# When the first remainders of q and k are loaded, and by which queue, and four norms a group sooner, in a fused attention and MLP kernel

## The chip, the core and the metric

The kernel runs on one core of one Trainium2 chip. The core has five engines that run side by side, each through its own instructions in order: TensorE (PE, matrix products into PSUM; its weight loads are listed apart as PEld), VectorE (DVE), ScalarE (ACT), GpSimd (POOL) and SyncE (SP, which here only issues transfers). Transfers between the chip's memory (HBM) and the on-chip memory are issued by SP, ACT or POOL and carried out by 16 DMA engines. The metric is the device time of one execution in microseconds (us). A profile shows one execution: its times count from the start of its span, and its lines name lines of the kernel (L184 is line 184).

## The reference

Attention over normalised q and k, and then a two-layer network over the joined heads. q, k and v have the shape (8 batches, 12 heads, 448 tokens, 64), in float32; `tau` is 0.1; the layers are 768 to 2048 and back.

```python
q_n = q / (np.linalg.norm(q, axis=-1, keepdims=True) + 1e-06)
k_n = k / (np.linalg.norm(k, axis=-1, keepdims=True) + 1e-06)
scores = np.matmul(q_n, k_n.transpose(0, 1, 3, 2)) / tau
scores = scores - np.max(scores, axis=-1, keepdims=True)
attn = np.exp(scores)
attn = attn / (np.sum(attn, axis=-1, keepdims=True) + 1e-09)
attn_out = np.matmul(attn, v)
x = attn_out.transpose(0, 2, 1, 3).reshape(B * S, H * D)
h = x @ w_in
out = np.maximum(0.01 * h, h) @ w_out
```

## The kernel before, in words

**Tiles.** The unit of attention is a slot: a pair of heads of one batch, six slots to a batch, 48 in all, numbered `s`. The 448 tokens of a head are 384 in three tiles of 128 (the main part) and a remainder of 64. The main part of q or k of a pair is one load of 192 KB. The remainder of q goes to partitions 0 to 63 of a fourth tile and that of k to partitions 64 to 127, in loads of 32 KB each, so that q with both remainders is 128x512 and k 128x384. The six slots of the first batch have a buffer of their own, `raw0`, filled by `load_first` (`part` 0 is the main part at L129, 1 the remainder at L134; `s0` and `n` say which slots). Later slots take turns in four buffers named `qk`, filled by `load_qk` with four loads on SP (L144, L145, L147 twice).

**One slot's way.** Squares (`squares`, L184, on POOL; for the first two slots on ACT and DVE, L522 to L533), sums over 64 (`sums`, L195, DVE), square roots as exp of half a log (`roots`, L202 and L203, ACT; L205 adds a small number for the first two slots), the norm (`normalise`: L214, L215 and two L219 on DVE, which write `qn` in bf16), transposes to `qkT` (on PE, L233, with a copy at L257 or L547 up to slot 9; from slot 10 by a DMA transpose on SP, L251), scores (L276, PE), exp (L288, ACT, into `pe`, and `pr` for the remainders of two slots together). Four heads then form a quarter `j` of a batch: `totals` (sums of exp by products with ones, L316; L329 and L330 invert them), `products` with v (L316, weights `v_b`, `v_rem`), `scale` (L351) into `xT`.

**The network.** `xT` of two batches is worked off in chunks of 384 and 512 tokens. `first` makes one of 16 groups of hidden columns (L374, PE) and its activation (L381, ACT, `hT`); `two_groups` and `second` make the output products (L453, L411).

**The order.** It is written out by hand: each engine runs the instructions in the order in which the program calls them, and waits by semaphores. First the loads are issued, then 22 products of ones (`fill`, L503) keep PE at work. A loop over the six slots of the first batch follows (L553 on): within step `s` come scores of `s`, sums of `s + 2`, the norm of `s + 1`, loads, `hold`, squares of `s + 3`, loads of weights and v, transposes of `s + 1`. `hold` (L510) is a copy of one element on POOL: POOL waits there for what it reads, and what POOL issues afterwards is issued no earlier. The first one reads the main part of k of slot 1. The software loads on POOL are `load_w_in` (L106), `load_w_out` (L113), `load_v` (L162, `v_b`) and `load_v_rem` (L169).

**Loads and semaphores.** The loads issued by SP and ACT take eight semaphores in turn. A load that takes one in use waits, on its engine, until the earlier load has landed; in the program before, the first to do so is the q load of slot 3, which waits for that of slot 0.

**The later part.** For each batch `b`: `visit` (output products of chunk `b`, with the scores of the next batch's slots in between; it begins with the scores of the remainders, for the slots 1 and 3 of that batch and their predecessors), `attend_batch(b + 1)`, loads of v, and `firsts(b + 1, 0, between)`. `between` says which sums and norms come ahead of which of the 16 groups. `norm(s)` is roots, norm, transposes, the load of slot `s + 4`, a hold and the squares of slot `s + 2`. The case `b == 0` has a list of its own, for slots 12 to 15 and the sums of 16.

Of the kernel before, what the change touches and what calls it, by code (L numbers as in the profile page):

```python
# [16 lines left out]
def kernel(  # L17
# [10 lines left out]
    nc = tc.nc  # L28
# [38 lines left out]
    gp = nc.gpsimd  # L67
# [50 lines left out]
    def main(x, b, h0, nh):  # L118
        return x[b, h0 : h0 + nh, 0:MAIN].rearrange("h (p t) d -> p h t d", t=3)

    raw0 = cpool.tile([128, NPAIR, 2, 7, D], F32, name="raw0")
    raw = {s: (raw0[:, s, :, 0:4], raw0[:, s, :, 4:7]) for s in range(NPAIR)}

    def load_first(eng, x, part, s0, n):

        h0, i = 2 * s0, 0 if x is q else 1
        if part == 0:
            dst = raw0[:, s0 : s0 + n, :, 4 * i : 4 * i + 3]
            eng.dma_start(  # L129
                out=dst.rearrange("p s h t d -> p (s h) t d"), in_=main(x, 0, h0, 2 * n)  # L130
            )
        else:
            dst = raw0[64 * i : 64 * i + 64, s0 : s0 + n, :, 3]
            eng.dma_start(  # L134
                out=dst.rearrange("p s h d -> p (s h) d"),
                in_=x[0, h0 : h0 + 2 * n, MAIN:S].rearrange("h p d -> p h d"),
            )

    def load_qk(s):
        if s >= NSLOT:  # L140
            return
        b, h0 = s // NPAIR, 2 * (s % NPAIR)
        both = ldp.tile([128, 2, 7, D], F32, name="qk")
        nc.sync.dma_start(out=both[:, :, 0:3], in_=main(q, b, h0, 2))  # L144
        nc.sync.dma_start(out=both[:, :, 4:7], in_=main(k, b, h0, 2))  # L145
        for i, x in enumerate((q, k)):
            nc.sync.dma_start(  # L147
                out=both[64 * i : 64 * i + 64, :, 3],
                in_=x[b, h0 : h0 + 2, MAIN:S].rearrange("h p d -> p h d"),
            )  # L150
        raw[s] = (both[:, :, 0:4], both[:, :, 4:7])
# [5 lines left out]
    def load_v(j):  # L157
        if j >= B * NQ:
            return
        b, jj = divmod(j, NQ)  # L160
        vb[j] = vbp.tile([128, 4, 3, D], BF16, name="v_b")
        gp.dma_start(out=vb[j], in_=main(v, b, 4 * jj, 4))  # L162

    def load_v_rem(b, parts=slice(0, 4)):
        if b >= B:
            return
        x = vrb[b % 2].rearrange("p j g d -> p (j g) d")
        for lo, h0, h1 in ((0, 0, 2), (64, 2, 6), (0, 6, 10), (64, 10, 12))[parts]:
            gp.dma_start(  # L169
                out=x[lo : lo + 64, h0:h1], in_=v[b, h0:h1, MAIN:S].rearrange("h p d -> p h d")  # L170
            )
# [3 lines left out]
    def squares(s, engs=(gp, gp)):  # L175
        if s >= NSLOT:
            return
        tiles = []
        for x, eng, name in zip(raw[s], engs, ("sq0", "sq1")):
            sq = sqp.tile(list(x.shape), F32, name=name)  # L180
            if eng is nc.scalar:
                nc.scalar.activation(sq, x, func=AF.Square)
            else:
                eng.tensor_tensor(sq, x, x, op=ALU.mult)  # L184
            tiles.append(sq)
        sqs[s] = tiles

    def sums(s, parts=(0, 1)):
        if s >= NSLOT:
            return  # L190
        if s not in ss:
            ss[s] = smp.tile([128, 14], F32, name="ss")
        for i in parts:
            o = ss[s][:, 0:8] if i == 0 else ss[s][:, 8:14]
            nc.vector.tensor_reduce(  # L195
                o.rearrange("p (h t) -> p h t", h=2), sqs[s][i], axis=AX.X, op=ALU.add
            )

    def roots(s):
        if s >= NSLOT:  # L200
            return
        nc.scalar.activation(ss[s], ss[s], func=AF.Ln, bias=tiny)  # L202
        nc.scalar.activation(ss[s], ss[s], func=AF.Exp, scale=0.5)  # L203
        if s < 2:
            nc.scalar.activation(ss[s], ss[s], func=AF.Identity, bias=eps)  # L205
# [3 lines left out]
    def normalise(s):  # L209
        if s >= NSLOT:  # L210
            return
        r = smp.tile([128, 14], F32, name="r")
        if s >= 2:
            nc.vector.tensor_scalar_add(ss[s], ss[s], 1e-6)  # L214
        nc.vector.reciprocal(r, ss[s])  # L215
        qn[s] = qnp.tile([128, 7, 2, D], BF16, name="qn")
        for x, lo, hi, r0 in ((raw[s][0], 0, 4, 0), (raw[s][1], 4, 7, 8)):
            nt = hi - lo
            nc.vector.tensor_tensor(  # L219
                qn[s][:, lo:hi],  # L220
                x.rearrange("p h t d -> p t h d"),
                r[:, r0 : r0 + 2 * nt].rearrange("p (h t) -> p t h", h=2)
                .unsqueeze(3).to_broadcast([128, nt, 2, D]),
                op=ALU.mult,
            )
# [19 lines left out]
    def transposes(s):  # L245
        if s >= NSLOT:
            return
        dst = qtp.tile([128, 7, 128], BF16, name="qkT")
        qkT[s] = dst.rearrange("p t c -> p (t c)")
        if s >= DMA_FROM:  # L250
            nc.sync.dma_start(  # L251
                out=dst, in_=qn[s].rearrange("p t h d -> p (t h d)"), transpose=True
            )
            return
        tp = transposed()
        one(tp, s, 0, 7)
        nc.vector.tensor_copy(out=dst, in_=tp)  # L257
# [102 lines left out]
    def chunk_cols(c):  # L360
        return (0, MAIN) if c % 2 == 0 else (MAIN, 512)
# [111 lines left out]
        load_first(nc.scalar, k, part, 0, 1)  # L473
    load_first(nc.sync, q, 0, 1, 1)
    load_first(nc.scalar, k, 0, 1, 1)
    for x in (q, k):
        load_first(gp, x, 1, 1, 5)
    for s, n in ((2, 1), (3, 1), (4, 2)):
        for x in (q, k):
            load_first(nc.sync, x, 0, s, n)  # L480
    tiny = cpool.tile([128, 1], F32, name="tiny")
    nc.vector.memset(tiny, 1e-18)
    eps = cpool.tile([128, 1], F32, name="eps")
# [26 lines left out]
    def hold(x):  # L510
        seen = smp.tile([128, 1], F32, name="seen")
        gp.tensor_copy(out=seen, in_=x)  # L512

    hold(raw[1][1][:, 0, 0, 0:1])
    load_v_rem(0, slice(0, 2))


# [35 lines left out]
    for s in range(NPAIR):  # L553
        j = s // 2 - 1 if s >= 2 else None
        even = s % 2 == 0
        n = s + 2 if s + 2 < NPAIR else None
# [91 lines left out]
    def attend_batch(b):  # L648
        attend_two(b * NQ)
        attend(b * NQ + 2)  # L650


    def norm(s, transposed=True):
        if s >= NSLOT:
            return
        roots(s)
        normalise(s)
        if transposed:
            transposes(s)
        if not 8 <= s < 12:  # L660
            load_qk(s + 4)
        elif s >= 10:
            load_qk(s + 2)
        hold(qn[s][:, 6, 0, 0:1])
        squares(s + 2)
# [51 lines left out]
    for b in range(B):  # L717
        tokens = chunk_cols(b)[1] // 128
        if b == B - 1:
            for ts in range(tokens):  # L720
                for half in range(2):
                    second(b, ts, half)
            break
        order = [((ts, 0), (ts, 1)) for ts in range(tokens)]
        if b == 0:
            order = [((0, 0), (1, 0)), ((2, 0), (0, 1)), ((1, 1), (2, 1))]
        visit(b, order, tokens - 1, three if tokens == 3 else four)
        ready += tokens - 1
        attend_batch(b + 1)
        for j in range((b + 2) * NQ, (b + 3) * NQ):  # L730
            load_v(j)
        load_v_rem(b + 2)
        s = ready
        between = {0: [lambda s=s: norm(s)], 1: [lambda s=s: sums(s + 1)]}
        if b == 0:
            between = {
                0: [lambda: load_qk(14), lambda: load_qk(15)],
                1: [lambda: sums(12)], 2: [lambda: norm(12)], 3: [lambda: sums(13)],
                5: [lambda: norm(13), lambda: sums(14)], 8: [lambda: norm(14), lambda: sums(15)],
                10: [lambda: norm(15)], 13: [lambda: sums(16)],  # L740
            }
            ready += 4
        elif tokens == 3:
            between.update({
                4: [lambda s=s: norm(s + 1), lambda s=s: sums(s + 2)],
                7: [lambda s=s: norm(s + 2), lambda s=s: sums(s + 3)],
                10: [lambda s=s: norm(s + 3)], 13: [lambda s=s: sums(s + 4)],
            })
            ready += 4
        else:  # L750
            between.update({
                4: [lambda s=s: norm(s + 1)], 5: [lambda s=s: sums(s + 2)],
                8: [lambda s=s: norm(s + 2)], 12: [lambda s=s: sums(s + 3)],
            })
            ready += 3
        firsts(b + 1, 0, between)
# [35 lines left out]
```

## Time and profile before

| | us |
|---|---|
| median of 3 runs | 414.03 (413.63 to 415.51) |
| the profiled execution | 414.07 |
| its span | 412.30 |
| PE busy | 400.8 (97%) |
| ACT busy | 260.4 (63%) |
| DVE busy | 192.5 (47%) |
| POOL busy | 140.3 (34%) |
| PE busy in the first 9.4 us | 7.69 (22 products of ones) |
| PE busy from 9.4 to 34.6 | 20.46 of 25.2 |
| PE busy from 34.6 to 103.2 | 67.84 of 68.6 |
| PE busy from 103.2 to 412.3 | 304.84 of 309.1 |

A line of the timeline reads: start, duration, engine, line, operation, written tile <- read tiles, shapes, number of equal instructions merged into the line, and in brackets how long the engine had been idle and what ended it. SPq and ACTq are the engines' own queues of instructions, where transfers are issued. A line of the view of waits reads: engine, its line, what it waited for, us in total, times, and the longest. A line of DMA issues gives the size and the median time from issue to landing.

### The profile page before, as it was taken

Reading aid. Unit: us, or ns where it says so; the run is one execution under the profiler, and the core shown is the slowest. Engines: PE = TensorE matmul, PEld = TensorE weight load, DVE = VectorE, ACT = ScalarE, POOL = GpSimd, SP = SyncE. Lnnn points to the kernel's source line nnn. Section 1 sums busy time; section 2 is a strip of 40 time slices with the busy share of each in tenths; the row PEclk is TensorE's granted clock in tenths of the full one; section 3 lists DMA queues with packets and bytes.
Section 4 is the critical chain, followed back from the end, with each engine's and each line's share of the span. In section 5 each row is a group of like instructions: output and inputs, shape, how many; then the busy total and the mean of one; then the engine's idle time right before and its main releaser. Section 6 shows DMA issues by size and latency. Waiting matters only on the chain.

```text
span 412.3 us, 10091 instructions
## 1 busy us (share of the span) xinstructions
PE 400.8 (97%) x4088; PEld 213.4 (52%) x4099; DVE 192.5 (47%) x412; ACT 260.4 (63%) x448; POOL 140.3 (34%) x214
## 2 busy tenths in 40 slices
PE   8689999999999999999999999999999999999996
PEld 3234655544555555544555555544555555544564
DVE  5876953465543635255352726157262644130021
ACT  3897588555875569755785469845775559844300
POOL 3984474534231514055140634054231530000000
PEclk9999999999999999999999999999999999999999
DMA  7999999778585958387485966586376843210023
GB/s 192 255 218 209 218 157 211 164 136 161 130 191 101 129 120 171 101 115 152 99 189 121 125 145 124 130 114 149 83 190 137 113 89 63 62 41 2 0 76 78
DMA packets 103615, 54.21 MB, mean 131 GB/s; under 512 B 69424, under 2 KB 98480, under 8 KB 103568
## 3 DMA queue, kind: packets, MB, share of 16 engines
q1 hardware_dynamic: 77488, 40.91, 42.6%
q0 software_dynamic: 25232, 12.13, 22.9%
q8 instruction: 32, 0.52, 0.5%
q10 hardware_dynamic: 848, 0.52, 0.5%
q14 instruction: 15, 0.12, 0.1%
HBM read 45.61 MB, written 11.01 MB: 137 GB/s over the span
## 4 chain that ended last, share of the span: by engine, by line
PE 92%; DMA 3%; DVE 1%; ACT 1%; issue 1%; SPq 0%; POOL 0%; POOLq 0%
PE ps L374 35%; PE ps L453 31%; PE ps L316 12%; PE ps L276 8%; PE ps L411 5%; DMA raw<-in_q_dram 3%; PE ps L303 1%; ACT pe L288 1%; DVE qn L219 1%; DMA qkT<-qn 1%; PE ps L233 1%; POOL sq L184 0%; ACT pr L288 0%; SPq L134 0%; DVE qkT L257 0%
## 5 line engine op out<-in xcount | busy, mean ns | idle before, releaser
L374 PE MATMUL ps<-xT,w_in_sb 128*128 128x384 bf16 (+1 forms) x760 | 147.3, 352 | 0.4
L453 PE MATMUL ps<-w_out_sb,hT 64*128 64x384 bf16 x1536 | 142.7, 323 | 0.0
L288 ACT ACTIVATE pe<-ps 128x896 bf16<-128x896 f32 x144 | 123.6, 918 | 20.6 <-PE ps L276 18.5
L381 ACT ACTIVATE hT<-ps 128x384 bf16<-128x384 f32 (+1 forms) x128 | 67.7, 543 | 72.4 <-PE ps L374 71.3
L374 PEld LDWEIGHTS <-w_in_sb 128*128 128x128 bf16 x768 | 74.1, 98 | 71.3 <-issue 3.4
L453 PEld LDWEIGHTS <-hT 64*128 64x128 bf16 x1536 | 73.6, 94 | 54.8 <-issue 3.2
L184 POOL TENSOR_TENSOR sq<-qk 128x512 f32<-128x512 f32 x84 | 77.1, 938 | 12.7 <-DMA qk<-in_k_dram 12.0
L463 DVE COPY osb<-ps 128x384 f32<-128x384 f32 x48 | 24.5, 552 | 77.9 <-PE ps L453 44.7
L276 PE MATMUL ps<-qkT 64*128 64x448 bf16 (+1 forms) x384 | 54.1, 354 | 4.3 <-ACT pe L288 2.3
L195 DVE TENSOR_REDUCE ss<-sq 128x6 f32<-128x384 f32 (+1 forms) x95 | 54.4, 610 | 0.7 <-POOL sq L184 0.6
L512 POOL CAST seen<-qn 128x1 f32<-128x1 bf16 x48 | 8.9, 186 | 130.5 <-DVE qn L219 124.3
L219 DVE TENSOR_TENSOR qn<-qk,r 128x512 bf16<-128x512 f32 x84 | 50.2, 639 | 1.7 <-DMA qk<-in_k_dram 0.3
L214 DVE TENSOR_SCALAR ss<-ss 128x14 f32<-128x14 f32 x46 | 9.7, 211 | 66.2 <-ACT ss L203 66.1
L162 POOL DMA_DIRECT2D v_b<-in_v_dram x24 | 18.5, 773 | 59.5 <-PE ps L316 59.5
L351 DVE TENSOR_TENSOR xT<-ps,rb 128x448 bf16<-128x448 f32 x48 | 27.7, 619 | 23.4 <-ACT rb L330 23.4
L316 PE MATMUL ps<-pe,v_b 128*32 128x448 bf16 x576 | 31.9, 353 | 0.0
L276 PEld LDWEIGHTS <-qkT 64*128 64x128 bf16 (+1 forms) x384 | 16.8, 96 | 24.5 <-issue 10.8
L329 ACT ACTIVATE rb<-ps 128x448 f32<-128x448 f32 x24 | 12.9, 538 | 23.3 <-PE ps L316 23.3
L417 DVE COPY osb<-ps 128x384 f32<-128x384 f32 (+1 forms) x9 | 4.6, 513 | 36.6 <-issue 22.6
L288 ACT ACTIVATE pr<-ps 128x896 bf16<-128x896 f32 x24 | 21.4, 922 | 0.2 <-PE ps L276 0.2
L316 PEld LDWEIGHTS <-v_b 128*32 128x32 bf16 x576 | 15.2, 97 | 12.0 <-DMA v_b<-in_v_dram 0.3
L411 PE MATMUL ps<-w_out_sb,hT 128*128 128x384 bf16 (+1 forms) x144 | 21.0, 308 | 0.0
(51 smaller groups left out, 197.3 us busy)
## 6 DMA issues: line engine op xcount, KB each, us to landing
qk<-in_q_dram SPq DMA_DIRECT2D x42, 192.0 KB, 3.2
qk<-in_k_dram SPq DMA_DIRECT2D x42, 192.0 KB, 3.1
out_dram<-osb SPq DMA_DIRECT2D x30, 192.0 KB, 2.9
v_b<-in_v_dram POOLq DMA_DIRECT2D x24, 192.0 KB, 4.8
out_dram<-osb SPq DMA_DIRECT2D x12, 384.0 KB, 3.2
w_in_sb<-in_moe_w_in_dram POOLq DMA_DIRECT2D x4, 768.0 KB, 11.6
w_out_sb<-in_moe_w_out_dram POOLq DMA_DIRECT2D x1, 1536.0 KB, 21.5
w_out_sb<-in_moe_w_out_dram POOLq DMA_DIRECT2D x4, 384.0 KB, 22.4
```

What stands on the lines that cost most here:

```text
L184: eng.tensor_tensor(sq, x, x, op=ALU.mult)
L195: nc.vector.tensor_reduce(o.rearrange("p (h t) -> p h t", h=2), sqs[s][i], axis=AX.X, op=ALU.add)
L219: nc.vector.tensor_tensor(qn[s][:, lo:hi], x.rearrange("p h t d -> p t h d"), r[:, r0 : r0 + 2 * nt].rearrange("p (h t) -> p t h", h=2) .u ...
L276: nc.tensor.matmul(out=out[:, a, :S], lhsT=x[rows, c0:c1], rhs=x[rows, 0:S], start=True, stop=True,)
L288: nc.scalar.activation(out=dst, in_=sc[:, :, :S], func=AF.Exp, scale=inv_tau)
L316: nc.tensor.matmul(out=x[32 * g : 32 * g + 32, :S], lhsT=weights(g, ki) if ki < 3 else rem(g), rhs=pe[s][:, ki, a, :] if ki < 3 else pr[j] ...
L351: nc.vector.tensor_tensor(xT[m][:, 2 * jj + e, half * S : (half + 1) * S], pos.pop((j, e))[:, :S], rbs[j], op=ALU.mult,)
L374: nc.tensor.matmul(out=pm[:, :n], lhsT=w_in_sb[:, kt, m * 128 : (m + 1) * 128], rhs=xT[c // 2][:, kt, c0 : c0 + n], start=(kt == 0), stop= ...
L381: nc.scalar.activation(out=hT[c][:, m, :n], in_=pms.pop((c, m))[:, :n], func=AF.Prelu, alpha=0.01)
L411: nc.tensor.matmul(out=po2[:, :n], lhsT=hT[c][:, m, ts * 128 : (ts + 1) * 128], rhs=w_out_sb[:, m, lo : lo + n], start=(m == 0), stop=(m = ...
L453: last[i] = nc.tensor.matmul(out=po2[:, i, :HALF], lhsT=hT[c][rows, m, ts * 128 : (ts + 1) * 128], rhs=w_out_sb[rows, m, half * HALF : (ha ...
L463: nc.vector.tensor_copy(out=osb[c, ts][:, half * HALF : (half + 1) * HALF], in_=po2[:, i, :HALF])
```

## The change

Three things are edited.

- The remainders of slots 1 to 5 were two loads on POOL, the first instructions there. Slot 1's are now two loads on SP, behind the main part of q of slot 1 and ahead of the main parts of slots 2 to 5. Those of slots 2 to 5 are two loads on POOL behind a hold.
- The first hold reads slot 0's fourth tile, which holds the remainders of both q and k, in place of k of slot 1. Behind it stand the two new loads, and then the `v_rem` loads as before.
- In the list for `b == 0`, sums of 12 move from ahead of group 1 to group 0, the norm of 12 from 2 to 1, sums of 13 from 3 to 1, the norm of 13 and sums of 14 from 5 to 4, the norm of 14 and sums of 15 from 8 to 7, and the norm of 15 from 10 to 9.

```diff
     load_first(nc.sync, q, 0, 1, 1)
     load_first(nc.scalar, k, 0, 1, 1)
-    for x in (q, k):
-        load_first(gp, x, 1, 1, 5)
-    for s, n in ((2, 1), (3, 1), (4, 2)):
+    for part, s, n in ((1, 1, 1), (0, 2, 1), (0, 3, 1), (0, 4, 2)):
         for x in (q, k):
-            load_first(nc.sync, x, 0, s, n)
+            load_first(nc.sync, x, part, s, n)
...
-    hold(raw[1][1][:, 0, 0, 0:1])
+    hold(raw0[:, 0, 0, 3, 0:1])
+    for x in (q, k):
+        load_first(gp, x, 1, 2, 4)
     load_v_rem(0, slice(0, 2))
...
         if b == 0:
             between = {
-                0: [lambda: load_qk(14), lambda: load_qk(15)],
-                1: [lambda: sums(12)], 2: [lambda: norm(12)], 3: [lambda: sums(13)],
-                5: [lambda: norm(13), lambda: sums(14)], 8: [lambda: norm(14), lambda: sums(15)],
-                10: [lambda: norm(15)], 13: [lambda: sums(16)],
+                0: [lambda: load_qk(14), lambda: load_qk(15), lambda: sums(12)],
+                1: [lambda: norm(12), lambda: sums(13)], 4: [lambda: norm(13), lambda: sums(14)],
+                7: [lambda: norm(14), lambda: sums(15)], 9: [lambda: norm(15)],
+                13: [lambda: sums(16)],
             }
```

## The prediction

> **What bounds the kernel now.** I read the page first, then the idle time of TensorE, then the timeline of the two stretches that idle time points to. PE is busy 400.8 of 412.3 us, at a granted clock of 9 tenths or more in every slice, so a change can win only what PE idles. The view of waits, for PE alone, says when that is:
>
> ```profile
> PE ps L276 <- ACT pe L288: 2.3, 5, 1.1
> PE ps L503 <- DVE warm L486: 1.5, 1, 1.5
> PE ps L276 <- DVE qkT L257: 1.0, 2, 0.7
> PE ps L276 <- DMA qkT<-qn: 0.7, 1, 0.7
> ```
>
> The first three belong to the start, where q, k, v and the weights arrive and PE has little to do (the window sums give PE 28.2 busy us of the first 34.6). The last is one wait of 0.7 us near 103 us. After it PE has no gap over 0.05 us up to the last matmul, so what is won or lost in these two places moves the end by as much.
>
> The start, in the timeline:
>
> ```profile
> 1.28 0.91 POOL L134 DMA_DIRECT2D raw<-in_q_dram  x1 [0.83 <-POOLq L773]
> 2.19 0.74 POOL L134 DMA_DIRECT2D raw<-in_k_dram  x1
> 6.80 0.31 ACT L525 ACTIVATE sq<-raw 128x128 f32<-128x128 f32 x1 [2.25 <-DMA raw<-in_k_dram]
> 9.44 1.26 POOL L169 DMA_DIRECT2D v_rem<-in_v_dram  x2
> 10.82 1.85 POOL L184 TENSOR_TENSOR sq<-raw 128x512 f32<-128x512 f32 x2
> 13.38 0.80 POOL L162 DMA_DIRECT2D v_b<-in_v_dram  x1
> 18.38 0.18 POOL L512 CAST seen<-qn 128x1 f32<-128x1 bf16 x1 [0.27 <-DVE qn L219]
> 23.42 0.31 PEld L316 LDWEIGHTS <-v_b 128*32 128x32 bf16 x12 [0.27 <-DMA v_b<-in_v_dram]
> ```
>
> Three things are to be seen. ACT waits 2.25 us for the first pair's remainder (L525). GpSimd works nearly without a break from 10.82 on; its largest idle time until 25 us is 0.27. And the first products with v (23.42) already wait for `v_b`, which GpSimd issues at 13.38, behind the squares of the third pair. The issues of this stretch, KB and us to landing:
>
> ```profile
> raw<-in_q_dram POOLq DMA_DIRECT2D x1, 160.0 KB, 4.7
> raw<-in_k_dram POOLq DMA_DIRECT2D x1, 160.0 KB, 6.5
> raw<-in_q_dram SPq DMA_DIRECT2D x1, 32.0 KB, 3.7
> raw<-in_k_dram ACTq DMA_DIRECT2D x1, 32.0 KB, 5.4
> ```
>
> The second place, on SP and PE:
>
> ```profile
> 87.84 1.25 SPq L251 DMA_TRANSPOSE qkT<-qn  x1
> 91.70 1.26 SPq L251 DMA_TRANSPOSE qkT<-qn  x1
> 96.35 1.28 SPq L251 DMA_TRANSPOSE qkT<-qn  x1
> 100.21 1.26 SPq L251 DMA_TRANSPOSE qkT<-qn  x1
> 103.24 0.38 PE L276 MATMUL ps<-qkT 64*64 64x448 bf16 x4 [0.69 <-DMA qkT<-qn]
> ```
>
> These are the transposes of slots 12 to 15, each with four loads of q and k behind it on SP. From 87.84 to 103.94 SP does one after the other; the last lands 3.0 us after its issue, and PE waits 0.69.
>
> **The change, part by part.** The diff gives both remainders of the second pair to SyncE and none to ScalarE; I cost what it does.
>
> *The first pair's remainder* (pair 1 is slot 0, and so on). Two 160 KB loads leave the time before 8 us. Their company slows the others: the DMA view gives 291 GB/s for 2.5 to 3.7 us, with SP's and ACT's queues alone, and 229 GB/s for 4.9 to 8.0, with the software queue beside them. The q remainder lands at 1.26 + 3.7 = 4.97 now, and k's at 1.30 + 5.4 = 6.7. Alone, k's should land like q's, so the pair is there between 4.97 and 6.7; I take 5.1, nearer the first, since the cause of the difference is gone. L525 then starts at 5.2 instead of 6.80. But the short reduce behind it (L527, 7.15) also waits for the long one on DVE, which ends at 5.75 + 0.54 = 6.29: it gains 0.86. The roots and the first norm follow by that (8.67 becomes 7.8). The transposes do not: PE's 22 fills last until 1.52 + 7.69 = 9.21, and the transposes start at 9.42 now. The second pair's squares (slot 1; ACT L532, 9.17) wait for loads that now land near 6.5, so its roots at 11.26 are set by the copies and sums around the transposes; going down DVE and ACT row by row they start at about 10.65. This side gains 0.6 us, and no more, because of the fills.
>
> *SP's queue.* Two issues of 0.60 to 0.75 us go ahead of the loads of pairs 3 to 6. Eight semaphores serve SP's and ACT's loads in turn, so the third pair's q load waits for the first pair's (landed 4.0, now issued near 4.1 instead of 2.69) and its k load for the first q remainder (5.0 instead of 3.20). With at most 5 us to landing they are there by 10, and are needed by GpSimd at 10.82. I cost this at nothing; the wait below covers it, and without it the cost would be 0 to 0.3.
>
> *GpSimd.* Its hold moves from 9.20 (the second pair's k) to 5.2. Behind it stand the remainders of pairs 3 to 6 (two loads of 128 KB, 0.74 us each from the row at 2.19), the two `v_rem` loads, which thereby start at 6.9 instead of 9.44, then the hold for the first norm (10.67; free to run at 9.1). So the second remainder load is issued at 5.2 + 0.2 + 0.74 = 6.15. It was issued at 2.19. The squares of the third pair need both. Time to landing is bounded by rows: 4.5 us is the least that a software load needed in this stretch (`v_rem`, 16 KB, issued at 9.44 beside SP's loads) and 6.5 the most (this load itself, with two hardware queues beside it and 160 KB). That gives 10.65 to 12.65. The new place has one hardware queue beside it, as `v_rem` has, but 128 KB; the 32 KB `v_rem` behind the first took 5.0, so I take 5.1: landed at 11.25, squares at 11.35, 0.53 later than now.
>
> The Trainium skill, page "DMA: Bandwidth & Descriptors", section "Anatomy of one DMA — SWDGE (gpsimd) path", fits 2.0 us plus bytes over 436 GB/s; by it 128 KB land in an estimated 2.3 us, at 8.45, the squares wait only for the first norm, and the sum is that of the early rival below. The trace does not agree: 4.7 and 6.5 us for 160 KB here.
>
> Everything on GpSimd follows its squares: the next ones 14.31 − 10.82 = 3.49 later, the `v_b` issue 2.56 later. The next loop (norm, hold, squares, sums, norm) can take back the 0.27 idle at 18.38. But `v_b` has no slack: it lands 10.0 us after its issue and PE waits for it. It would land 0.53 later, less what it gains as SP's loads are further ahead (from 20 to 23.5 us they move 0.51 MB beside the software queue's 0.26 MB). That relief is between 0 and 0.8; I take 0.2, because w_in's 768 KB ahead of it are slowed little by SP (10.9% of the engines from 16 to 20). The 0.6 us of the other side is thus lost, and the start ends 0.33 us **later**.
>
> *The norms.* The sums of slot 12 already run on DVE at 82.20, before either place, and are free. The roots of slot 12 go ahead of the second group's activation on ACT: 85.06 instead of 85.54, 0.48 sooner. Their norm and transpose follow (87.84 becomes 87.36), since SP is idle before. From there both chains keep their steps: DVE needs about 3.66 us a slot, SP 3.86. Asking for slots 13 to 15 a group sooner adds nothing, because they wait for DVE and SP, not for a place. ACT may now wait up to 1 us for sums ahead of an activation; that is covered by the PSUM banks, eight of them at 1.3 us a group. So the last transpose lands 0.48 sooner and PE waits 0.21. Bounds are 0 and 0.69; 0.48 is the one that rests on rows.
>
> *Sum.* The profiled execution took 414.07 us (span 412.30, 1.77 around it), 0.04 above the median of three. 414.07 + 0.33 − 0.48 = 413.92: **413.9 us**.
>
> **The rivals.**
> - *GpSimd late.* The second remainder load needs its 6.5 us again. Squares at 12.75, 1.93 later; `v_b` moves by that less 0.2, and with the norms 414.07 + 1.73 − 0.48 = 415.3: slower. It decides from squares later than about 11.5. For it speaks that this very load took so long behind its twin; against it, that it is smaller and ACT's queue is empty by then. To be over 0.5% slower it would take a landing near 13.7, or a load issued at 7 instead of 6.15.
> - *GpSimd in time.* Landing below 10.6. The squares start between 9.4 and 10.7, `v_b` has no part in it any more, and the start keeps the 0.6 of the ACT and DVE side: 414.07 − 0.6 − 0.48 = 413.0. For it speaks that the first of the two took 4.7 us with 160 KB. This is what the page's fit would make of it.
> - *The norms do nothing.* SP has to wait at one of its steps, as at 93.58 to 94.06 now, or the roots of slot 12 find no room: 414.07 + 0.33 = 414.4.
>
> **How the numbers follow.** Chances: forecast 0.42, late 0.24, in time 0.24, norms without effect 0.10. From 413.0 to 415.3, with a tenth for the spread of the runs (413.63 to 415.51), I give 412.8 to 415.4; the forecast's own range is 413.4 to 414.5. Of this kernel 0.5% (2.07 us) is about what a measurement can tell from no change. Faster than 411.96 would need more than both places hold (0.6 + 0.69): 0.03. Slower than 416.1 is the end of the late case: 0.07. The rest, 0.90, lies within.
>
> **What would show it.** In the profile of the changed kernel: L525 near 5.2 without its 2.25 us wait; the first norm near 7.8; the transposes right behind the fills. POOL's first L184: at 11.35, waiting for a remainder, by the forecast; near 9.4 in time; at 12.7 late. The first products with v: a wait for `v_b` near 23.8. The transpose of slot 12 near 87.4 + 0.33 and PE's wait before the first scores of that visit 0.2 instead of 0.69. I am wrong if POOL's squares start before 10.8, if PE waits at 23 us for something else, or if SP's chain breaks up.

## The result, and the profile after

The changed kernel takes 416.21 us (median of 8 runs, 415.26 to 417.10) against 414.71 of the kernel before, run beside it (8 runs, 413.63 to 415.51): ratio 1.0039, 95% interval 1.0024 to 1.0054. So it is a little slower, by about 0.4%, and beyond the upper end of the predicted range, 415.4. The profiled execution took 416.25, span 414.5: 2.18 more than the profiled one of before. The medians differ by 1.50 only, because the profiled execution of before, 414.07, was 0.64 below the median of its kernel. In the profiles both places lost.

The start, in the timeline of the kernel after (the engines together, in order of time):

```profile
5.57 0.31 ACT L525 ACTIVATE sq<-raw 128x128 f32<-128x128 f32 x1 [1.02 <-DMA raw<-in_k_dram]
5.62 0.18 POOL L510 COPY seen<-raw 128x1 f32<-128x1 f32 x1 [4.31 <-DMA raw<-in_k_dram]
6.19 0.88 POOL L134 DMA_DIRECT2D raw<-in_q_dram  x1 [0.38 <-issue]
7.06 0.71 POOL L134 DMA_DIRECT2D raw<-in_k_dram  x1
...
12.98 1.82 POOL L184 TENSOR_TENSOR sq<-raw 128x512 f32<-128x512 f32 x2 [3.77 <-issue]
...
14.84 0.55 DVE L195 TENSOR_REDUCE ss<-sq 128x6 f32<-128x384 f32 x1 [2.43 <-POOL sq L184]
15.31 0.61 DVE L257 COPY qkT<-ps 128x896 bf16<-128x896 bf16 x1
15.55 0.80 POOL L162 DMA_DIRECT2D v_b<-in_v_dram  x1
15.98 0.93 PE L276 MATMUL ps<-qkT 64*128 64x448 bf16 x4 [3.17 <-DVE qkT L257]
...
25.34 0.31 PEld L316 LDWEIGHTS <-v_b 128*32 128x32 bf16 x12 [0.28 <-DMA v_b<-in_v_dram]
...
36.52 0.66 PE L374 MATMUL ps<-xT,w_in_sb 128*128 128x384 bf16 x3
```

L525 starts at 5.57 instead of 6.80 (5.2 was forecast). But GpSimd, which had its squares (L184) at 10.82, now stands idle for 3.77 us and has them at 12.98. The 3.77 are put down to "issue", with no releaser; the loads show what it waited for. These are the issues from 0 to 9 us of the kernel after (KB, us to landing):

```profile
raw<-in_q_dram POOLq DMA_DIRECT2D x1, 128.0 KB, 4.6
raw<-in_k_dram POOLq DMA_DIRECT2D x1, 128.0 KB, 5.8
raw<-in_q_dram SPq DMA_DIRECT2D x2, 32.0 KB, 3.8
raw<-in_k_dram ACTq DMA_DIRECT2D x1, 32.0 KB, 4.2
```

The second one, issued at 7.06, landed at 12.85, and the squares began 0.13 us later. Behind them come `v_b` (15.55 instead of 13.38; it is in use at 25.34 instead of 23.42) and the first product of the network (L374: 36.52 instead of 34.59, 1.93 later). A second thing is new: DVE waits 2.43 us for the squares (L195), and the copy of the second pair's `qkT` (L257) stands behind that on the same engine, so PE waits 3.17 us at 15.98. PE's waits of the kernel after (us in total, times, longest):

```profile
PE ps L276 <- DVE qkT L257: 3.5, 2, 3.2
...
PE ps L276 <- DMA qkT<-qn: 1.1, 1, 1.1
```

The last line is the second place: 1.1 us, where 0.7 stood and 0.2 was forecast. On SP and PE there, in the kernel after:

```profile
89.28 1.26 SPq L251 DMA_TRANSPOSE qkT<-qn  x1
...
93.11 1.26 SPq L251 DMA_TRANSPOSE qkT<-qn  x1
94.91 0.40 SPq L144 DMA_DIRECT2D qk<-in_q_dram  x1
95.38 1.81 SPq L145 DMA_DIRECT2D qk<-in_k_dram  x1
...
98.65 1.27 SPq L251 DMA_TRANSPOSE qkT<-qn  x1
...
102.50 1.26 SPq L251 DMA_TRANSPOSE qkT<-qn  x1
...
105.52 0.38 PE L276 MATMUL ps<-qkT 64*64 64x448 bf16 x4 [1.06 <-DMA qkT<-qn]
```

With the start 1.93 later, the transpose of slot 12 comes at 89.28, where 87.84 + 1.93 = 89.77 would have been without the edit: 0.49 is won, as forecast. Slot 13 keeps it (93.11). Then the load at 95.38 takes 1.81 us, and the step from slot 13 to slot 14 is 5.54 us instead of 4.65: 0.89 is lost. PE's wait is therefore 1.06 instead of 0.69. In the kernel before, the same load took 0.37, and what made the step 4.65 were the 0.48 us ahead of it and the 1.10 of the next one:

```profile
93.06 0.52 SPq L144 DMA_DIRECT2D qk<-in_q_dram  x1
94.06 0.37 SPq L145 DMA_DIRECT2D qk<-in_k_dram  x1
94.49 1.10 SPq L147 DMA_DIRECT2D qk<-in_q_dram  x1
```

The view of the DMA queues of the kernel after, for 95 to 98.5 us (GB/s in 40 slices; queue, kind: packets, MB, share), shows what else ran then:

```profile
GB/s 211 205 211 202 173 337 6 0 0 0 0 70 79 158 97 88 167 246 342 325 220 211 97 35 9 18 18 9 9 18 26 9 53 176 132 167 149 184 290 334
...
q8 instruction: 1, 0.02, 2.3%
q14 instruction: 1, 0.01, 1.8%
```

Two transfers of instructions, 16 KB on q8 and 8 KB on q14, began at 95.50 and 95.46, and right then SP's loads moved next to nothing for 0.4 us. In the kernel before they began at 94.24 and 96.44, apart.

So the two profiles account for their difference: +1.93 at the start, +0.37 at the second place, in all 2.30, and 2.18 was measured. Between the medians there is only 1.50 to account for, and one profile of each kernel does not tell at which place it is less.

The granted clock of TensorE differs too. In the profile of before it is 1.00 from 8 to 34 us; in that of the changed kernel it is 0.91 from 14 to 16 us, 0.50 from 16 to 18 and 0.74 from 18 to 20. That is not what made the start late there: `v_b` is issued 2.57 us behind the squares (2.56 before), and from its landing to L374 both profiles take 11.2 us.

### The profile page after: what moved, and what is told of

Read it like the earlier page. It is cut to its first block, busy times and chain, and to the rows that moved or that the text cites. A ratio compares the mean times of both kernels' runs of the same rounds, so it can differ in the third digit from the quotient of the medians.

```text
span 414.5 us, 10095 instructions
## 1 busy us (share of the span) xinstructions
PE 400.8 (97%) x4088; PEld 213.3 (51%) x4099; DVE 191.6 (46%) x412; ACT 260.2 (63%) x448; POOL 140.4 (34%) x214
## 4 chain that ended last, share of the span: by engine, by line
PE 92%; DMA 3%; POOL 2%; issue 1%; ACT 1%; DVE 0%; POOLq 0%
PE ps L374 35%; PE ps L453 30%; PE ps L316 12%; PE ps L276 8%; PE ps L411 5%; PE ps L303 1%; DMA raw<-in_q_dram 1%; POOL sq L184 1%; DMA raw<-in_k_dram 1%; DMA qkT<-qn 1%; ACT pe L288 1%; PE ps L233 1%; POOL v_rem L169 0%; DVE qn L219 0%; POOL v_b L162 0%
## 5 line engine op out<-in xcount | busy, mean ns | idle before, releaser
L374 PE MATMUL ps<-xT,w_in_sb 128*128 128x384 bf16 (+1 forms) x760 | 147.3, 352 | 0.4
L374 PEld LDWEIGHTS <-w_in_sb 128*128 128x128 bf16 x768 | 74.1, 98 | 71.3 <-issue 3.4
L184 POOL TENSOR_TENSOR sq<-qk 128x512 f32<-128x512 f32 x84 | 77.2, 939 | 13.8 <-DMA qk<-in_k_dram 12.6
L195 DVE TENSOR_REDUCE ss<-sq 128x6 f32<-128x384 f32 (+1 forms) x95 | 54.5, 610 | 4.6 <-POOL sq L184 4.4
```

Of the source, the lines that this page charges most:

```text
L195: nc.vector.tensor_reduce(o.rearrange("p (h t) -> p h t", h=2), sqs[s][i], axis=AX.X, op=ALU.add)
L374: nc.tensor.matmul(out=pm[:, :n], lhsT=w_in_sb[:, kt, m * 128 : (m + 1) * 128], rhs=xT[c // 2][:, kt, c0 : c0 + n], start=(kt == 0), stop= ...
```

## The experiments

Two things had to be told apart at the start, and one thing at the second place. The letters in the expectations stand for these theories. **G**: GpSimd's hold delays its second software load, and squares, `v_b` and PE follow. **V**: `v_b` is late because w_in's 768 KB lie ahead of it in the same software queue. **F**, later made sharper as **C**: fetches of instructions hold up SP's loads at the second place; by C it is where the two fetches fall in relation to each other, and the one on q14 is SP's and moves with the number of SP's instructions. The rivals are named with each run.

All runs in one table. "Squares" is the start of GpSimd's first L184, "v_b" its landing, "L374" the first product of the network, "step" the time from slot 13's transpose to slot 14's on SP, "wait" PE's wait at the second place (us, one profiled execution each, whose time is in the column "profiled"); the ratio is to the kernel before on the same chip, whose medians were 414.70, 414.84 and 414.64 in the three sets.

| run | median | profiled | ratio (95%) | squares | v_b | L374 | step | wait |
|---|---|---|---|---|---|---|---|---|
| before | 414.71 | 414.07 | | 10.82 | 23.37 | 34.59 | 4.65 | 0.69 |
| after | 416.21 | 416.25 | 1.0039 (1.0024 to 1.0054) | 12.98 | 25.30 | 36.52 | 5.54 | 1.06 |
| start_only | 416.03 | 416.34 | 1.0035 (1.0022 to 1.0049) | 13.18 | 25.61 | 36.83 | 4.80 | 0.84 |
| norms_only | 414.32 | 414.39 | 0.9987 (0.9975 to 0.9998) | 10.79 | 23.53 | 34.75 | 5.29 | 0.85 |
| norms_split | 415.62 | 415.31 | 1.0026 (1.0008 to 1.0045) | 10.95 | 24.45 | 35.66 | 5.50 | 1.00 |
| third_on_sp | 413.54 | 413.30 | 0.9980 (0.9970 to 0.9990) | 9.31 | 23.40 | 34.61 | 4.10 | 0.15 |
| no_hold | 414.67 | 415.14 | 0.9993 (0.9980 to 1.0006) | 10.46 | 24.28 | 35.50 | 5.53 | 0.99 |
| norms_sp2 | 414.85 | 415.67 | 1.0002 (0.9989 to 1.0015) | 11.16 | 24.56 | 35.78 | 5.62 | 1.07 |
| norms_sp4 | 414.68 | 415.81 | 0.9995 (0.9983 to 1.0007) | 11.61 | 25.82 | 37.04 | 4.09 | 0 |
| third_v_first | 413.04 | 412.68 | 0.9953 (0.9938 to 0.9968) | 9.89 | 18.79 | 33.58 | 4.63 | 0.54 |
| v_first | 414.42 | 415.12 | 0.9996 (0.9987 to 1.0005) | 11.19 | 17.52 | 35.55 | 4.79 | 0.75 |
| after_v_first | 416.38 | 416.14 | 1.0051 (1.0039 to 1.0063) | 12.92 | 18.99 | 36.37 | 5.55 | 1.07 |
| after_hold_main | 414.58 | 414.53 | 0.9997 (0.9989 to 1.0006) | 10.57 | 23.55 | 34.76 | 5.56 | 1.09 |

Three regularities hold. Where w_in is issued ahead of `v_b`, L374 comes 11.21 or 11.22 us after `v_b` has landed, in all ten rows. And from L374 to PE's last instruction it is 373.1 us plus the wait, in all thirteen (before: 408.40 − 34.59 = 373.81 = 373.12 + 0.69; after: 410.68 − 36.52 = 374.16 = 373.10 + 1.06). Last, slot 12's transpose is issued 53.24 or 53.25 us after L374 with the old list (three rows) and 52.75 or 52.76 with the new one (ten). The two places, then, are all that these profiles differ in up to the end of PE's work, and the new list wins 0.49 us for slot 12 each time. A profiled execution can lie up to 1.1 us from the median of its kernel (norms_sp4), so the columns on the right do not add up to the medians.

**start_only: the loads alone.** The changed kernel with the norms as before.

```diff
-                0: [lambda: load_qk(14), lambda: load_qk(15), lambda: sums(12)],
...
+                0: [lambda: load_qk(14), lambda: load_qk(15)],
+                1: [lambda: sums(12)], 2: [lambda: norm(12)], 3: [lambda: sums(13)],
+                5: [lambda: norm(13), lambda: sums(14)], 8: [lambda: norm(14), lambda: sums(15)],
+                10: [lambda: norm(15)], 13: [lambda: sums(16)],
```

> The loads are as in the changed kernel, the norms of slots 12 to 15 stand where they stood. Theory G (GpSimd's hold delays the second remainder load of pairs 3 to 6 and the whole start with it): the first squares on POOL start at about 13.0 instead of 10.8, the first products with v wait for v_b at about 25.3, and PE enters the long part 1.9 us later than before. Theory F (two more instructions on SP move SP's own fetch of instructions into the loads behind the transpose of slot 13): PE's wait before the first scores of the second visit is 1.4 to 1.6 us instead of 0.69, since nothing takes 0.48 off. Together about 2.7 us slower than before. Rival N (the norms' new places cost the time there): the wait stays at 0.69 and the kernel is 1.9 us slower.

GpSimd's loads are issued at 6.05 and 6.92 and land at 10.69 and 13.05; squares at 13.18, L374 2.24 later than before. The time, 416.03, cannot be told from that of the whole change. The loss lies in this part. What F said of the second place was a miss: the wait is 0.84, not 1.4 to 1.6, with the two fetches 0.34 us apart.

**norms_only: the list for `b == 0` alone**, in the kernel before.

```diff
-                0: [lambda: load_qk(14), lambda: load_qk(15)],
...
+                0: [lambda: load_qk(14), lambda: load_qk(15), lambda: sums(12)],
+                1: [lambda: norm(12), lambda: sums(13)], 4: [lambda: norm(13), lambda: sums(14)],
+                7: [lambda: norm(14), lambda: sums(15)], 9: [lambda: norm(15)],
...
```

> The loads are as before, only the norms stand a group sooner. Theory F and the prediction: the transpose of slot 12 is issued 0.48 us sooner and that of slot 15 too, PE's wait before the first scores of the second visit is 0.2 us instead of 0.69, and the kernel is about 0.5 us faster. Rival N: the wait is about 1.06 us as in the changed kernel, and the kernel is 0.3 to 0.4 us slower.

The transpose of slot 12 is 0.33 sooner than before (87.51), in a profile whose L374 is 0.16 later, so 0.49 is won again. But the step to slot 14 is 5.29, one SP load (L147) takes 1.75, and PE waits 0.85, where about 0.2 was expected. So the late start was not needed for the stall, and the first form of F falls. The median is 0.4 us below before, and the interval just excludes no change; that is nearly the 0.5 that was expected, but the wait in the profile is longer and not shorter, so where it was won is not shown.

**norms_split: two more instructions on SP.** Norms as in the change; the main loads of slots 4 and 5 become four loads.

```diff
-    for s, n in ((2, 1), (3, 1), (4, 2)):
+    for s, n in ((2, 1), (3, 1), (4, 1), (5, 1)):
```

> As the one with the norms alone, and the main loads of pairs 5 and 6 are four loads on SP instead of two, so that SP has two more instructions ahead of everything that follows, as in the changed kernel, with the same bytes. Theory F: SP's fetch of instructions falls into the loads behind the transpose of slot 13 again, the transpose of slot 15 is issued about 0.9 us later than with the norms alone, and PE's wait there is about 1.0 us. Rival (the fetch has no part; the late start or the new loads moved it): the wait is the same 0.2 us as with the norms alone. The start itself may move by up to 0.3 us either way.

The fetch on q14 came at 94.61, that on q8 at 94.56, the step was 5.50 and the wait 1.00. But the start moved by more than the 0.3 us that was allowed for: `v_b` landed 1.1 us later than before. So the run is a poor test of the second place by its time.

**third_on_sp: the changed kernel, with the third pair's remainders taken from GpSimd.** The hold stays.

```diff
-    for part, s, n in ((1, 1, 1), (0, 2, 1), (0, 3, 1), (0, 4, 2)):
+    for part, s, n in ((1, 1, 1), (1, 2, 1), (0, 2, 1), (0, 3, 1), (0, 4, 2)):
...
-        load_first(gp, x, 1, 2, 4)
+        load_first(gp, x, 1, 3, 3)
```

> As the changed kernel, but the remainders of pair 3 are two loads on SP as well, and GpSimd's two loads behind its hold are those of pairs 4 to 6. Theory G: POOL's first squares no longer wait for a software load; they start between 9.0 and 10.0 us, the first products with v come 1.5 to 2.5 us earlier than in the changed kernel (at 22.5 to 23.8), and the start is 0 to 0.9 us ahead of the kernel before. Rival (the start is late because SP's own loads are late, by the two issues ahead of them): squares at about 12 or later, and no more than 0.5 us gained on the changed kernel. SP has two more instructions again, so the wait near 103 us is open: 0.2 to 1.1 us.

GpSimd's two loads are later still (7.29 for the second), and it no longer matters: the squares start at 9.31, 1.51 ahead of before, as G has it; by the rival (SP's own loads late) they would have come at 12 or later. Yet `v_b`, issued at 11.87 instead of 13.38, lands at 23.40, as late as before, and L374 stays where it was. The lines of GpSimd and of PE's weight loads in this run:

```profile
9.31 1.88 POOL L184 TENSOR_TENSOR sq<-raw 128x512 f32<-128x512 f32 x2
11.08 0.81 POOL L106 DMA_DIRECT2D w_in_sb<-in_moe_w_in_dram  x1
11.87 0.80 POOL L162 DMA_DIRECT2D v_b<-in_v_dram  x1
...
23.44 0.31 PEld L316 LDWEIGHTS <-v_b 128*32 128x32 bf16 x12 [1.14 <-DMA v_b<-in_v_dram]
```

What the profile shows to be won is at the second place, where the wait fell to 0.15. That is 0.54 of the 1.16 us between the medians; the rest is not located.

**no_hold: the loads of pairs 3 to 6 as GpSimd's first instructions.** The rest of the change stays, the hold too, ahead of `v_rem`.

```diff
+    for x in (q, k):
+        load_first(gp, x, 1, 2, 4)
     for part, s, n in ((1, 1, 1), (0, 2, 1), (0, 3, 1), (0, 4, 2)):
...
-    for x in (q, k):
-        load_first(gp, x, 1, 2, 4)
     load_v_rem(0, slice(0, 2))
```

> As the changed kernel, but GpSimd issues the remainders of pairs 3 to 6 first of all, as the kernel before did, and not behind the hold (the hold stays ahead of the v_rem loads). Theory G (the hold is what makes the start late): the two loads are issued near 1.3 and 2.2 us, POOL's first squares start between 9.2 and 10.9 us, the first pair's remainder lands late again (6 to 6.8), and the kernel loses the 1.9 us of the start: within 0.3% of the kernel before. Rival (the second pair's loads ahead on SP make it late): squares at 12 or later, slower by 1 us or more.

The two loads land at 5.77 and 6.89, and the squares are at 10.46. In exchange the first pair's remainders land at 6.96 and 7.13 again, and L525 starts at 7.22. The loss of the change is gone (414.67, no difference from before that can be measured), and so is what it was to win.

**norms_sp2 and norms_sp4: SP instructions added that move no data.** The norms as in the change, the loads as before; two or five more instructions on SP, which only wait for early memsets. The diff of norms_sp2 is shown; four memsets are listed in it and nine in norms_sp4, and several waits become one instruction, so that SP has 386 and 389 instructions in the traces instead of 384.

```diff
+    set_before = []
...
-    nc.vector.memset(tiny, 1e-18)
+    set_before.append(nc.vector.memset(tiny, 1e-18))
...
+    for made in set_before:
+        tc.add_manual_dep(
+            nc.sync.nop().ins, made.ins.name,
+            mybir.DependencyInfo(mybir.DependencyClass.Sync, mybir.DependencyReason.DATA),
+            reason="one more instruction on SyncE",
+        )
```

> As the one with the norms alone, with two more instructions on SP near 10 us that only wait for memsets long done, so that no load differs. In all profiles so far SP's own fetch of instructions (8 KB) begins at about the 83rd instruction of its program. With two more, that is the k load of slot 17, as in the changed kernel. Theory C (the fetches of SP and of PE, 16 KB, fall together and hold up SP's issue of loads): from the transpose of slot 13 to that of slot 14 SP takes 5.3 to 5.7 us, as in the changed kernel (5.54), against 3.86 undisturbed, and PE waits 0.8 to 1.1 us near 103. Rival (it is another load or landing that holds SP up): no more than 4.7 us and a wait of 0.2 to 0.7.

> The same with five more instructions on SP (nine waits for memsets, joined to five instructions). SP's 83rd instruction is then the transpose of slot 13 itself, ahead of PE's fetch, as in the run with the third pair on SP. Theory C: from the transpose of slot 13 to that of slot 14 3.9 to 4.3 us, PE waits 0 to 0.25 us near 103, and the kernel is 0.5 to 0.9 us faster than with the norms alone. Rival: as with the norms alone, 5.3 us and 0.85.

With two more, the fetch on q14 begins 2.63 us after slot 13's transpose (3.08 without them), 0.24 from the one on q8, and SP stalls the longest of all runs:

```profile
94.17 0.40 SPq L144 DMA_DIRECT2D qk<-in_q_dram  x1
94.64 1.90 SPq L145 DMA_DIRECT2D qk<-in_k_dram  x1
96.58 0.66 SPq L147 DMA_DIRECT2D qk<-in_q_dram  x1
```

With five more it begins 0.20 us after that transpose (94.25) and 2.45 ahead of the other (96.70). The same loads in norms_sp4:

```profile
94.05 1.26 SPq L251 DMA_TRANSPOSE qkT<-qn  x1
95.40 0.53 SPq L144 DMA_DIRECT2D qk<-in_q_dram  x1
95.99 0.46 SPq L145 DMA_DIRECT2D qk<-in_k_dram  x1
...
98.14 1.27 SPq L251 DMA_TRANSPOSE qkT<-qn  x1
```

The step is 4.09 and PE's wait is gone. That agrees with C for the second place. For the time it was a miss: both medians are those of before, and the profile of norms_sp4 has a start that is 2.45 later (`v_b` issued at 14.17, landed at 25.82). Part of it began ahead of anything added: k's first remainder, issued by ACT at 1.30 as before, landed at 7.60 instead of 6.72, and squares and `v_b` were issued 0.79 later. The other part is `v_b` itself, which took 11.65 us instead of 9.99. The execution was a slow one of its kernel (415.81, median 414.68).

**third_v_first: third_on_sp with `v_b` issued ahead of w_in.**

```diff
-    load_w_in(0)
     load_v(0)
+    load_w_in(0)
```

> As the run with the third pair's remainders on SP, and GpSimd issues the first v_b load ahead of the first w_in load instead of behind it. Theory V (v_b lands late because 768 KB of w_in lie ahead of it in the same queue, whenever it is issued): v_b lands before 18 us, PE's wait of 0.87 at 23.44 goes, and the kernel is 0.6 to 1.0 us faster than that run, about 412.7. w_in lands about 1 to 2 us later, at 22 to 23, and is first needed at 34. Rival (v_b is late because of SP's loads beside it): it lands no earlier than 21 and the kernel gains under 0.3 us.

`v_b`, issued at 11.68, lands at 18.79 instead of 23.40 (before 18 was expected); PE no longer waits for it, and L374 is at 33.58, 1.01 sooner than before:

```profile
9.89 1.85 POOL L184 TENSOR_TENSOR sq<-raw 128x512 f32<-128x512 f32 x2 [1.07 <-DMA raw<-in_q_dram]
11.68 0.81 POOL L162 DMA_DIRECT2D v_b<-in_v_dram  x1
12.48 0.75 POOL L106 DMA_DIRECT2D w_in_sb<-in_moe_w_in_dram  x1
...
22.40 0.31 PEld L316 LDWEIGHTS <-v_b 128*32 128x32 bf16 x12 [0.20 <-issue]
...
33.58 0.82 PE L374 MATMUL ps<-xT,w_in_sb 128*128 128x384 bf16 x4
```

At 413.04 us, ratio 0.9953 (0.9938 to 0.9968), it beats both kernels.

**v_first and after_v_first: the same swap alone, in the kernel before and in the changed one.**

> The kernel before with one line moved: v_b of the first batch is issued ahead of w_in. Theory V (v_b lands late because w_in's 768 KB lie ahead of it in the same software queue): v_b lands by 20 instead of 23.4, the wait for it is gone, and the start gains what it cost, 0.3 to 0.6: median 0.3 to 0.6 below before, 414.2 to 414.5. Rival (the 1.8 us that the version with the third pair's remainders on SyncE and v first gained come from v_b alone): about 413. If the ACT and DVE side and the squares are needed for that gain, the first place is right.

> The changed kernel with v_b issued ahead of w_in. Squares of the third pair as in the changed kernel, near 13 (12.5 to 13.4), v_b landed by 22.5. Theory of the squares (PE gets its third pair late, whatever v_b does, as squares, sums, norm, transposes follow one another): the start is still 1.3 to 2.0 later than before, PE waits about 3 us near 16 for qkT, and the time is 415.6 to 416.3. Theory of v_b (as in the prediction: only the load of v_b hands GpSimd's delay to PE): the start is at most 0.3 later and the time 414.2 to 414.9.

In the kernel before, `v_b` lands at 17.52, and nothing is won that can be measured (ratio 0.9996, 0.9987 to 1.0005), where V expected 0.3 to 0.6 us. The gain of third_v_first does not come from `v_b` alone. In the changed kernel the swap helps as little: `v_b` lands 6 us sooner, PE does not wait for it, and L374 is only 0.15 sooner.

```profile
12.92 1.82 POOL L184 TENSOR_TENSOR sq<-raw 128x512 f32<-128x512 f32 x2 [3.81 <-issue]
14.69 0.81 POOL L162 DMA_DIRECT2D v_b<-in_v_dram  x1
...
15.91 0.93 PE L276 MATMUL ps<-qkT 64*128 64x448 bf16 x4 [2.56 <-DVE qkT L257]
...
36.37 0.82 PE L374 MATMUL ps<-xT,w_in_sb 128*128 128x384 bf16 x4
```

So the squares hand their delay to PE by two ways of nearly the same length: through `v_b`, and through the loop of squares, sums, norm and transposes. With `v_b` out of the way, L374 follows the squares by 23.45 (here), 23.69 (third_v_first) and 24.36 us (v_first); in the kernel before it follows them by 23.77 with `v_b` in the way. Of the versions tried, only the one that shortens both has L374 clearly sooner. The 24.36 of v_first is not a clean figure: in that profile the granted clock is 0.50 from 14 to 20 us, and the chain that ended last lies on PE from 15.35 to 20.09. In after_v_first it is as low there, but the chain runs through GpSimd and DVE.

**after_hold_main: the changed kernel, with its hold on data that land sooner.**

```diff
-    hold(raw0[:, 0, 0, 3, 0:1])
+    hold(raw0[:, 0, 0, 0, 0:1])
```

> The changed kernel with its first hold on the main part of q of the first pair (landed at 4.0) instead of the remainder (5.5). The hold is at 4.1, GpSimd's two loads are issued at 4.6 and 5.5 (instead of 6.19 and 7.06). Theory G (what counts is when the second of them is issued): landed at 10.1 to 11.3, 4.6 to 5.8 after its issue, squares at 10.2 to 11.4, so 1.6 to 2.8 sooner than in the changed kernel, and the time 1.3 to 2.3 below it: 414.0 to 414.9. Rival (the earlier loads are slowed by SyncE's, or slow the first pair's remainder again, as when they were issued first of all): second load landed after 12 or L525 after 6.2, and the time above 415.2.

```profile
4.12 0.18 POOL L510 COPY seen<-raw 128x1 f32<-128x1 f32 x1 [2.81 <-DMA raw<-in_q_dram]
4.24 0.88 POOL L134 DMA_DIRECT2D raw<-in_q_dram  x1
5.11 0.71 POOL L134 DMA_DIRECT2D raw<-in_k_dram  x1
...
10.57 2.27 POOL L184 TENSOR_TENSOR sq<-raw 128x512 f32<-128x512 f32 x2 [1.77 <-DMA raw<-in_k_dram]
```

The second load is issued 1.95 us sooner than in the changed kernel and lands 2.42 sooner, at 10.43, the squares are 2.41 sooner, L374 is 1.76 sooner, and the median is 1.63 lower. L525 keeps its gain (5.36). This is the change with nothing but the hold moved, and with it the issue of the two loads and of the `v_rem` loads behind them. It takes back nearly the whole loss at the start. The low clock stays (in all 11 executions the mean granted clock is 0.996 or less, as in all eight of the changed kernel), so the low clock alone does not cost the 1.5 us. The wait at the second place stays (1.09), with both fetches 0.05 us apart.

## Why the prediction was wrong

**The places and the mechanism at the start were right, one time was not.** PE's idle time at the start and the one wait near 103 us are indeed where the profiles differ. "Everything on GpSimd follows its squares" held to 0.01 us: `v_b` is issued 2.57 behind them, as 2.56 was taken. The relief for `v_b` behind a later issue was taken as 0.2 and is 0.24 (9.75 us to landing instead of 9.99). With the true start of the squares the same sum gives 2.16 − 0.2 = 1.96, and 1.93 was measured in the profiles.

**The step that failed is "the second remainder load is issued at 5.2 + 0.2 + 0.74 = 6.15 … I take 5.1: landed at 11.25, squares at 11.35".** It was issued at 7.06 and landed at 12.85. Four terms were too small. The hold ran at 5.62 instead of 5.2, because k's remainder landed at 5.48 and not at 5.1. Behind the hold GpSimd stood 0.38 us before its first load, which was left out. The first of the two loads took 0.88, where the row of the second (0.74) was used; the row of the first, at 1.28, said 0.91. Together that is 0.92 us. The landing took 5.8 us instead of 5.1, within the bounds of 4.5 to 6.5. The late rival took 6.5 us on an issue at 6.15 and so had the squares at 12.75; what happened was 5.8 on one at 7.06, and 12.98. "A load issued at 7" is what the prediction asked for to be over 0.5% slower; it came, and the kernel is 0.4% slower. The range for this step took both bounds of the landing and none for the issue.

The fit in the Trainium skill, page "DMA: Bandwidth & Descriptors", section "Anatomy of one DMA — SWDGE (gpsimd) path", 2.0 us plus bytes over 436 GB/s, gives an estimated 2.3 us for these loads. The measured 4.6 and 5.8 us, with SP's loads beside them, again do not agree; the early rival that would follow from it did not come.

**A way that was not named.** DVE's sums of the third pair wait for the squares, with the copy of the second pair's `qkT` behind them, and PE waits 3.17 us for that. The prediction gave the wait only to `v_b`. It changed no number, because both ways happen to be equally long, but it was wrong in what it would advise: after_v_first shows that moving `v_b` out of the way rescues 0.15 of the 1.93 us.

**The gain on the ACT and DVE side was larger than 0.6, and as lost.** The first pair's norm started 1.21 us sooner (7.46), and PE's transposes also 1.21 (8.21). The term "PE's 22 fills last until 9.21" was taken as fixed. PE's fills start every 0.43 us at first and every 0.22 later, and the step between came at 7.04 us in the profile before and at 5.34 in that after. It lay between 4.38 and 7.04 over the thirteen profiles, at 7.04 in after_v_first with the same starting loads. The moment belongs to the execution and not to the change. The Trainium skill, page "TensorE: Matmul & The Clock Gate", "Part 1: The HAM clock gate", has a free-running window of about 3.4 us after which a busy PE goes from half to full clock, so that the point of change varies from run to run, by ±0.5 us as the same part of the Trainium skill has it. The spread of 2.7 us here fits within such a window, but it is more than ±0.5 us. The granted clock reads 1.00 on both sides of the step, but that says nothing of the time before it: the traces' own record of the clock begins with the step, within 0.12 us of it in all thirteen. Later, between 11 and 21 us, seven of the profiles have one stretch at 0.50, of 3.41 or 6.83 us, and these lengths agree with one or two such windows.

**The two issues on SP cost nothing**, as said: the third pair's main parts were issued at 4.03 and 4.64 and landed by 8.49, and in no_hold, which has the two issues, the squares start at 10.46, no later than before.

**The norms: the first half of the step was right, the second fell.** Slot 12's transpose is 0.49 sooner in all ten profiles with the new list, where 0.48 was taken. "From there both chains keep their steps … SP 3.86" is what failed: SP's step to slot 14 took 5.54. The lines of before that were shown had the warning in them, for 96.35 − 91.70 is 4.65 and not 3.86, and the prediction passed over it. Only the rival "the norms do nothing" held an SP stall, with 0.10. Over the runs the stall goes with the distance of the two instruction fetches. Where they begin within 0.25 us of one another, the step is 5.50 to 5.62 (six runs); where they are 1.7 us or more apart, it is 4.09 to 4.65 (four runs); between, at 0.34 to 0.69, it is 4.79 to 5.29 (three).

**The base of the sum was low.** 414.07 is one execution, and 414.03 the median of three; the median of eight is 414.71. Of the 2.29 us between 413.92 and 416.21, 0.64 is this base, and 1.65 is the change, +1.50 instead of −0.15. The two profiles, 2.18 apart, show more than that because the profiled execution of before was one of the faster ones.

**What stays open.** How an instruction fetch keeps SP from issuing is not shown, only that the stall comes and goes with it. Nor is the second place proven in times: norms_only, norms_sp2 and norms_sp4 have waits of 0.85, 1.07 and 0 and medians of 414.32, 414.85 and 414.68, which do not follow the waits, and start_only and the whole change differ by less than their intervals. There is one profile of each kernel, and the start moves by up to 2.45 us between profiles with the same loads at the start (L374 at 34.59 in the kernel before and 37.04 in norms_sp4). The share of the start is shown in times too, by after_hold_main, though not its size: 1.63 us between two medians against 1.76 in the profiles.

## What to carry to other kernels

When a load is moved behind a wait, add up its issue time term by term (the wait itself, the dead time behind it, every load that is issued ahead on that engine, each by its own row) and give the issue bounds as well as the landing. An in-order engine that waits longer passes the delay to what stands behind it, so look for every engine that reads the late data: here `v_b` and DVE's sums led to the same PE, equally late, and only the version that shortened both had the network clearly sooner. A step of a chain that is longer than its neighbours in the trace of before has a cause, and a plan that moves the chain has to know it.

## What the runs showed of the hardware

- Instructions are fetched through the DMA queues while the kernel runs: in the kernel after 32 transfers on q8 (0.52 MB, 16 KB each) and 15 on q14 (0.12 MB, 8 KB each), which take 0.3 to 1.7 us near the second place. The one on q8 began 58.9 to 59.8 us after the first L374 in every run; that on q14 2.34 or 2.35 us after slot 13's transpose in all six runs with two more loads on SP than before, and 0.5 to 0.8 after it in the two with four more. In all thirteen traces the one on q14 began at SP's 81st to 84th instruction, so it looks like SP's fetch; that the one on q8 is PE's is inferred from its place behind L374 alone.
- In the software queue a load behind a large one landed behind it: 2.2 to 3.0 us after w_in in the ten runs with w_in ahead. `v_b` (192 KB) took 10.0, 9.8 and 11.5 us behind w_in's 768 KB, issued at 13.38, 15.55 and 11.87, and 7.1, 4.6 and 4.3 us ahead of it (third_v_first, v_first, after_v_first).
- The first software load behind a hold that GpSimd had to wait for was issued 0.38 or 0.39 us after the hold in five runs with the hold at 5.3 to 5.9; with the hold at 4.12 (after_hold_main) there was no such time, nor behind the hold at 9.20 in the kernel before (0.03), and behind the one at 7.28 in no_hold it was 0.28. What makes the difference is open.
